# Spectral FFN on one core: the first pair of batch 0 fed from SBUF, mix weights loaded ahead of the stores, weight bands decoded one pair later

## Chip, cores and metric

One core of one Trainium2 chip. The metric is the device time of one execution in microseconds (us), the median of several runs. Engines are named as in the profile: PE (TensorE), DVE (VectorE), ACT (ScalarE), POOL (GpSimd), SP (SyncE, which here only issues transfers).

## What is computed

Shapes: x is (8, 3008, 256) float32; w_r and w_i are 256 x 256; b_r and b_i have 256 elements; the two weights of the feed-forward part, 256 x 2048 and 2048 x 256, arrive as float64.

```python
X = rfft(x, axis=1);  Xr, Xi = X.real, X.imag
Yr = Xr @ w_r - Xi @ w_i + b_r
Yi = Xr @ w_i + Xi @ w_r + b_i
Yr, Yi = soft threshold of each with 0.01
y  = irfft(Yr + 1j * Yi, n=3008, axis=1)          # (8, 3008, 256)
h  = y.reshape(24064, 256) @ moe_w_in
out = (h * clip(h + 3, 0, 6) / 6) @ moe_w_out
```

## The kernel before

The transform of length 3008 = 64 x 47 is done in two steps. Stage 1 is a 47-point transform as matmuls with a constant matrix (f47), for all 64 residues; its result `a` goes to a scratch array in DRAM, scr1. The middle stage takes two of the 24 frequencies at a time (a "pair", `g`, 12 in all), reads their 128 rows (64 residues, real and imaginary) back from scr1, and does: `s2`, the 64-point transform; `s3`, the mix with w_r and w_i, where each operand is split into a high and a low part (`taken` makes X's high part on ACT, `remainder` the low part on DVE) and a first product adds the bias through a mean matrix; the threshold; `s5`, the inverse 64-point transform, whose result goes to scr2. The inverse 47-point transform and the feed-forward part follow in "units" of rows, with the middle stages of later batches spread between.

The two feed-forward weights arrive as pairs of 32-bit words of float64 and are decoded on chip in 16 "bands" (even: w_in, odd: w_out), each of 512 KB, in the steps exponent, clamped, sign, middle, rest, upper, lower or folded, sums_hi, sums_lo. `band()` issues a band's load on SP, `stage(n, what)` does one step of band n on DVE, ACT or POOL, and `tick` does the first two. EARLY bands are done during batch 0's middle stage, the rest in `later()`.

Around the change, the program does this:

- `first_stage1` (L325) handles batch 0 in seven sets, one of 96 rows and six of 120. Per set: sum and difference of the loaded halves on DVE and POOL (L347, L348), two products on PE (L358), a copy of each result to `a` (L371 on ACT, L369 on DVE), and a store of each to scr1 on SP's queue (L373, fourteen in all).
- Then w_r and w_i are loaded (L709, by the helper at L151), and half of the bias (L711); `next(mid)` twice issues the constants and data of pairs 0 and 1 (`constants`, `data`, L425 to L430): 64-point matrices `f`, and `bt`, which reads scr1 back.
- Bands 0 and 1 are loaded, `warm(8)` puts eight matmuls on zeros into PE's queue, ACT splits the mix weights (casts at L130, L724 to L726), and `run(mid)` runs all pairs of `first_middle` (L417).
- `later()` (L1153) is a generator that the main loop advances at a list of slots, `fill(q)`, four slots to a unit; `lay(segment(0, 2), ...)` and `stage1(1)` are placed by slots too.

Every engine runs its instructions in program order, and each has its own list; SP's list is the queue of nearly all transfers. A transfer is given one of eight semaphores in turn, and its issue waits until the transfer that used that semaphore before has landed (DMAHW0 to DMAHW7 in the rows below). In the main part a planner sets the order of the work from slots and data, so the order listing shows it better than the code.

Of the kernel before, what the change touches and what calls it, by code (L numbers as in the profile page):

```python
# [51 lines left out]

def constants():
# [23 lines left out]

    g64 = np.zeros((2, N1, 2, N1))
# [9 lines left out]
    for k in (0, N1 // 2):  # L88
# [5 lines left out]
        "f64": f(f64, P, NK * P),  # L94
        "g64": f(g64, P, P),
# [6 lines left out]
def spectral_ffn(ctx: ExitStack, tc: tile.TileContext, x, w_r, w_i, bias, w_in, w_out, f47, f64, g64, g64u, sgn, out):  # L102
# [183 lines left out]
    EARLY = 14  # L286
# [38 lines left out]
    def first_stage1():  # L325
# [24 lines left out]

        added(0)
        added(1)
        for i, (n1, n) in enumerate(sets):
# [63 lines left out]
    def first_middle():  # L417
# [13 lines left out]

        def s2(g):
            d, f = bt.pop(g)
# [12 lines left out]
        def taken(g):  # L446
            if g % 2 == 0:
                xt[g // 2] = space([P, 2, 2, 2, 2, P], F32R, "X", "gs")
            t = xt[g // 2][:, g % 2]
            nc.scalar.copy(out=t[:, 0], in_=ps_x[g].rearrange("p (h r c) -> p h r c", h=2, r=2))  # L450

        def remainder(g):
            t = xt[g // 2][:, g % 2]
            ps = ps_x.pop(g).rearrange("p (h r c) -> p h r c", h=2, r=2)
# [72 lines left out]
        constants(0)  # L527
        data(0)
        yield
# [3 lines left out]
        for g in range(NG + 2):  # L533
            n = g + 1 if g < NG else -9
# [11 lines left out]
            if g == 0:  # L546
                tick(g)
            elif g <= NG:
                stage(g, "clamped")
            stage(n - 3, "sums_hi")  # L550
            if g <= NG:
                stage(n - 3 if g < NG else g - 2, "upper")
            if g == 1:
                stage(0, "sign")
                stage(0, "middle")
                signed(0)
            if g:
# [4 lines left out]
            if g:  # L562
                on(signed, g)
                stage(n - 1, "middle")
# [9 lines left out]
            if g == NG + 1:  # L574
                tick(NG + 1, False)
                ahead.work(1)
                ahead.work(2)
                tick(NG + 2, False)
# [123 lines left out]
    next(first)  # L702
    warm(2)
# [9 lines left out]
    next(mid)  # L713
# [6 lines left out]
    warm(8)  # L720
# [432 lines left out]
    def later():  # L1153

        band()
        stage(EARLY, "exponent")
        stage(EARLY, "clamped")
        band()
        ahead.store()
        last = len(todo_bands) - 1  # L1160
        for steps in (
            ((12, "sums_hi"),),
            ((12, "sums_lo"),),
            ((14, "sign"), (14, "middle")),
# [5 lines left out]
            ((last, "exponent"), (last, "clamped")),  # L1170
            ((last, "sign"), (last, "middle")),
            ((last, "rest"), (last, "upper"), (last, "lower")),
# [168 lines left out]
```

## Time and profile before

| | us |
|---|---|
| median of 3 runs (2577.03 to 2577.23) | 2577.08 |
| the profiled execution, whole | 2578.3 |
| its span on the core | 2576.5 |
| PE busy in the span | 2558.8 (99%) |
| DVE busy | 1956.9 (76%) |
| ACT busy | 1964.1 (76%) |
| POOL busy | 729.2 (28%) |

How to read it: PE is busy in all but some 18 us of the span, and 91% of the chain of work that ended last is PE's. A busy sum does not say where the rest lies, so the rows further down are taken from single stretches. Times in rows are us from the span's start unless marked; "x4" after an operation is a count; "[0.52 <-PE ps_a L358]" means that the engine was idle 0.52 us before it and that PE's work on that tile ended the wait.

### The profile page before, as it was taken

The page shows a single profiled execution, that of the slowest core. Times are in us where ns is not written, and L with a number is a line of the kernel's source. Part 1 is how long each engine was busy: PE and PEld are TensorE (multiplying, and loading weights), DVE is VectorE, ACT ScalarE, POOL GpSimd, SP SyncE. Part 2 cuts the span into 40 slices and gives each one's busy share as a digit, 9 for nine tenths or more (in the row PEclk, how much of TensorE's full clock was granted, in tenths as well). Part 3 has the DMA queues.
Part 4 walks back from the last instruction along what each step waited for, and adds up shares of the span by engine and source line. Part 5 has one row for each costly group of instructions (what it writes and reads, how often), then busy time and mean ns, then how long its engine had stood idle before and what let it go on. Part 6 is the DMA issues. An engine that isn't in the chain of part 4 may idle for free.

```text
span 2576.5 us, 45563 instructions
## 1 busy us (share of the span) xinstructions
PE 2558.8 (99%) x16510; PEld 2291.1 (89%) x16510; DVE 1956.9 (76%) x3176; ACT 1964.1 (76%) x4329; POOL 729.2 (28%) x716
## 2 busy tenths in 40 slices
PE   9999999999999999999999999999999999999999
PEld 6788889889999989988899888998989999999998
DVE  6888877777777877777777777787777777766676
ACT  5777777777777777777777777777777777777877
POOL 2223422333133321433313432133411221121210
PEclk9999999999999999999999999999999999999999
DMA  8534422232122221222212322222311121110000
GB/s 278 170 99 137 126 73 74 84 89 76 54 83 79 89 80 51 81 83 82 79 55 78 90 87 67 69 73 85 90 62 53 55 73 49 37 32 25 20 17 17
DMA packets 147321, 199.75 MB, mean 78 GB/s; under 512 B 16319, under 2 KB 102039, under 8 KB 147095
## 3 DMA queue, kind: packets, MB, share of 16 engines
q1 hardware_dynamic: 147095, 196.83, 25.3%
q8 instruction: 130, 2.13, 0.3%
q14 instruction: 96, 0.79, 0.1%
HBM read 99.77 MB, written 74.97 MB: 68 GB/s over the span
## 4 chain that ended last, share of the span: by engine, by line
PE 91%; DVE 3%; ACT 3%; issue 2%; DMA 2%; POOL 0%; SPq 0%; ACTq 0%; DVEq 0%; POOLq 0%
PE po L137 38%; PE ps_a L137 25%; PE pb L137 19%; PE ps_a L868 3%; PE ps_a L754 3%; PE ps_a L471 1%; DVE gs L1096 1%; ACT gs L1095 1%; DMA qt<-scr 1%; ACT r L1090 1%; DVE h L1011 0%; DMA xin<-in_x 0%; DVE r L1092 0%; PE ps_a L506 0%; PE pb L438 0%
## 5 line engine op out<-in xcount | busy, mean ns | idle before, releaser
L137 PE MATMUL po<-gs,w_out_hi 128*128 128x512 f32 x3008 | 948.4, 396 | 1.0 <-DVE gs L1096 0.8
L1090 ACT ACTIVATE r<-h,three 128x512 f32<-128x512 f32 x750 | 541.4, 724 | 149.8 <-DVE h L1011 134.9
L1092 DVE SCALAR_TENSOR_TENSOR r<-r,h 128x1024 f32<-128x1024 f32 x375 | 491.2, 1310 | 210.0 <-ACT r L1090 209.0
L137 PEld LDWEIGHTS po<-gs,w_out_hi 128*128 128x128 f32 x3008 | 565.0, 188 | 87.3 <-DVE gs L1096 3.8
L137 PE MATMUL po<-gs,w_out_lo 128*128 128x512 f32 x1504 | 611.5, 407 | 0.2 <-ACT gs L1095 0.2
L1096 DVE TENSOR_TENSOR gs<-r,gs 128x1024 fp32r<-128x1024 f32 x375 | 479.0, 1277 | 162.3 <-ACT gs L1095 162.0
L1095 ACT CAST gs<-r 128x512 fp32r<-128x512 f32 x750 | 429.0, 619 | 176.5 <-DVE r L1092 171.9
L137 PE MATMUL pb<-yb,w_in_hi 128*128 128x256 f32 x3004 | 563.5, 280 | 0.0
L137 PEld LDWEIGHTS pb<-yb,w_in_hi 128*128 128x128 f32 x3004 | 460.0, 188 | 33.5
L131 POOL TENSOR_TENSOR yb<-T,yb 128x256 fp32r<-128x256 f32 x184 | 192.2, 1046 | 853.0 <-ACT yb L130 852.7
L137 PE MATMUL ps_a<-yb,w_in_hi 128*128 128x256 f32 x2252 | 432.0, 280 | 0.0
L137 PE MATMUL pb<-yb,w_in_lo 128*128 128x256 f32 x1502 | 423.0, 282 | 3.0 <-ACT u L1008 1.7
L1011 DVE TENSOR_TENSOR h<-ps_a,u 128x256 f32<-128x256 f32 x752 | 313.7, 417 | 132.8 <-PE ps_a L137 129.6
L137 PEld LDWEIGHTS ps_a<-yb,w_in_hi 128*128 128x128 f32 x2252 | 345.0, 188 | 17.0 <-DVE yb L131 0.2
L1008 ACT COPY u<-pb 128x256 f32<-128x256 f32 x752 | 278.9, 372 | 101.7 <-PE pb L137 100.1
L137 PE MATMUL ps_a<-yb,w_in_lo 128*128 128x256 f32 x1126 | 317.6, 282 | 4.0 <-DVE h L1011 3.7
L137 PEld LDWEIGHTS pb<-yb,w_in_lo 128*128 128x128 f32 x1502 | 282.8, 188 | 41.5 <-ACT p L1008 3.1
L137 PEld LDWEIGHTS po<-gs,w_out_lo 128*128 128x128 f32 x1504 | 283.5, 188 | 20.1 <-issue 2.2
L137 PEld LDWEIGHTS ps_a<-yb,w_in_lo 128*128 128x128 f32 x1126 | 211.6, 188 | 26.8 <-DVE h L1011 10.2
L1008 ACT COPY p<-pb 128x256 f32<-128x256 f32 x376 | 138.6, 369 | 37.3 <-PE pb L137 35.6
L1011 DVE TENSOR_TENSOR h<-ps_a,p 128x256 f32<-128x256 f32 x376 | 156.3, 416 | 2.5 <-ACT p L1008 1.9
L1067 ACT COPY h<-pb 128x256 f32<-128x256 f32 x376 | 141.6, 377 | 3.4 <-PE pb L137 3.3
(189 smaller groups left out, 3370.0 us busy)
## 6 DMA issues: line engine op xcount, KB each, us to landing
xin<-in_x SPq DMA_DIRECT2D x48, 512.0 KB, 3.6
bt<-scr SPq DMA_DIRECT2D x96, 256.0 KB, 3.2
scr<-pt SPq DMA_DIRECT2D x96, 256.0 KB, 2.0
out<-ot SPq DMA_DIRECT2D x93, 256.0 KB, 2.0
scr<-a SPq DMA_DIRECT2D x96, 240.0 KB, 2.5
qt<-scr SPq DMA_DIRECT2D x96, 240.0 KB, 3.4
zt<-tc SPq DMA_DIRECT2D x336, 64.0 KB, 2.0
f<-in_f SPq DMA_DIRECT2D x96, 128.0 KB, 2.9
```

Source lines behind the costliest of these rows:

```text
L131: (on or nc.vector).tensor_tensor(out=lo, in0=src, in1=hi.bitcast(F32), op=ALU.subtract)
L137: nc.tensor.matmul(out=ps, lhsT=a, rhs=b, start=start and n == 0, stop=stop and n == len(todo) - 1, skip_group_check=more,)
L471: nc.tensor.matmul(out=to, lhsT=x[:, xh, dh, which], rhs=w_s[w][wh][:, dh * D : (dh + 1) * D], start=False, stop=n == 2 and (which, dh) == ...
L754: nc.tensor.matmul(out=psv[:, dh, :, u, :], lhsT=data[:, u, dh * P : (dh + 1) * P], rhs=f[:, u, :], start=True, stop=True,)
L868: nc.tensor.matmul(out=ps[:, cs * w + g * rows : cs * w + (g + 1) * rows], lhsT=qt[:rows, cs, g, dh * P : (dh + 1) * P], rhs=f47_s[2][:row ...
L1008: nc.scalar.copy(out=t, in_=ps)
L1011: nc.vector.tensor_tensor(out=hs[i][:, u, half * H : (half + 1) * H], in0=ps, in1=keep.pop((i, n)), op=ALU.add)
L1067: nc.scalar.copy(out=hs[i][:, 1, :H], in_=pb)
L1090: nc.scalar.activation(out=r[:, u], in_=h[:, u], func=AF.Relu, bias=three, scale=1.0)
L1092: nc.vector.scalar_tensor_tensor(out=r, in0=r, scalar=6.0, in1=h, op0=ALU.min, op1=ALU.mult)
L1095: nc.scalar.copy(out=t[:, 0, u], in_=r[:, u])
L1096: nc.vector.tensor_tensor(out=t[:, 1], in0=r, in1=t[:, 0].bitcast(F32), op=ALU.subtract)
```

## The change

1. `first_rows()` gives the row order of the seven sets, `f64d` is a new constant of 256 KB with the 64-point matrices of the first pair in that order. `direct(i, a)` copies frequencies 0 and 1 of set i from `a` into the tile `bt_first`, both in SBUF, in two transfers on ACT's queue, issued behind ACT's first copy of the next set. `s2_first` multiplies them, each frequency on its own half of the rows and into its own PSUM bank, and X of pair 0 is made in two halves. Pair 0's constants and data are no longer loaded.
2. The loads of f_first (from f64d), w_r, w_i and half of the bias are issued ahead of the fourteen stores.
3. `warm(8)` becomes `warm(3)`. `tick` and the band steps in the middle stage come one pair later; EARLY goes from 14 to 13, so that `later()` starts with three bands' loads and has more steps and slots; the first slot of `stage1(1)` moves from 4 to 12.

```diff
         added(1)
+        behind_by_one = None
         for i, (n1, n) in enumerate(sets):
...
+                if behind_by_one is not None:
+                    direct(i - 1, behind_by_one)
+                    behind_by_one = None
                 dst = scr1[0][c, n1 : n1 + n].rearrange("(g j) k d -> (j k) g d", g=w // D)
                 nc.sync.dma_start(out=dst, in_=a[:, c].rearrange("p (g d) -> p g d", d=D))
+            behind_by_one = a
+            if i + 1 == len(sets):
+                direct(i, a)
...
+        def direct(i, a):
+            at, rows, w = first_rows()[i][0], *shapes[i]
+            for u in range(2):
+                src = a[u:rows:NK].rearrange("p c (g d) -> p c g d", d=D)
+                to = slice(u * N1 + at, u * N1 + at + rows // NK)
+                nc.scalar.dma_start(out=bt_first[to, :, : w // D], in_=src)
...
+        def s2_first():
+            pss = [room(True)[:, :D], ps_o.tile([P, 512], F32, name="po1")[:, :D]]
+            ps_x[0] = [ps.rearrange("p (h r c) -> p h r c", h=2, r=2) for ps in pss]
+            for dh in range(2):
+                for c in range(2):
+                    for gr in range(2):
+                        for u, ps in enumerate(pss):
+                            rows = slice(u * N1, u * N1 + (len(SEGS) - 1) * J + (0 if gr else SEGS[-1][1]))
+                            nc.tensor.matmul(
+                                out=ps[:, dh * P : (dh + 1) * P],
+                                lhsT=bt_first[rows, c, gr, dh * P : (dh + 1) * P],
+                                rhs=f_first[rows, 2 * c + gr, :],
...
-        constants(0)
-        data(0)
-        yield
...
-            if g == 0:
-                tick(g)
-            elif g <= NG:
-                stage(g, "clamped")
+            if g == 1:
+                tick(0)
+            elif 1 < g <= NG:
+                stage(g - 1, "clamped")
...
     next(first)
+    bt_first = space([P, 2, 2, D], F32, "bt_first", "z")
+    f_first = space([P, 4, P], F32, "f_first", "e")
+    nc.sync.dma_start(out=f_first, in_=f64d.rearrange("p (k c) -> p k c", c=P))
+    w_re, w_im = [loaded(w, P, 2 * D, n, "ot") for w, n in ((w_r, "w_r"), (w_i, "w_i"))]
+    nc.sync.dma_start(out=bias_s[: P // 2], in_=bias[: P // 2])
     warm(2)
...
     for i in range(len(SEGS)):
         next(first)
-    w_re, w_im = [loaded(w, P, 2 * D, n, "ot") for w, n in ((w_r, "w_r"), (w_i, "w_i"))]
...
-    nc.sync.dma_start(out=bias_s[: P // 2], in_=bias[: P // 2])
...
-    warm(8)
+    warm(3)
...
-    EARLY = 14
+    EARLY = 13
...
-        band()
-        stage(EARLY, "exponent")
-        stage(EARLY, "clamped")
-        band()
+        for _ in range(3):
+            band()
         ahead.store()
-        last = len(todo_bands) - 1
         for steps in (
+            ((12, "rest"), (12, "upper")),
             ((12, "sums_hi"),),
             ((12, "sums_lo"),),
+            ((13, "exponent"), (13, "clamped")),
+            ((14, "exponent"), (14, "clamped")),
+            ((13, "sign"), (13, "middle")),
...
-    for q in (0, 6, 8, 9, 11, 13, 15, 17, 18, 19, 20, 22, 45):
+    for q in (0, 3, 5, 6, 8, 9, 10, 11, 13, 14, 16, 17, 19, 20, 21, 23, 45):
...
-    for q in (4, 21, 23, 25, 27):
+    for q in (12, 21, 23, 25, 27):
```

How it moves instructions, at three places. The first is ACT in stage 1, from its first copy to the first cast of the mix weights, with the waits of each; before:

```order
L371 COPY a<-ps_a 96x256 [waits PE_49]
L371 COPY a<-ps_a 120x512 [waits PE_49] x4
L371 COPY a<-ps_a 120x512 [waits DMAHW1_49,DMAHW0_49,PE_49]
L371 COPY a<-ps_a 120x512 [waits DMAHW3_49,DMAHW2_49,PE_49]
L371 COPY a<-pb 120x512 [waits PE_49]
L130 CAST w_r_hi<-cst 128x512 [waits DMAHW6_49]
```

and now:

```order
L390 COPY a<-ps_a 120x512 [waits DMAHW1_49,DMAHW0_49,PE_49]
L367 DMA bt_first<-a 5x1024 [waits DMAHW6_49,DVE_49,Activation_49]
L367 DMA bt_first<-a 5x1024 [waits DMAHW1_49]
L390 COPY a<-ps_a 120x512 [waits DMAHW7_49,DMAHW4_49,PE_49]
L367 DMA bt_first<-a 5x1024 [waits DMAHW2_49,DVE_49,Activation_49]
L367 DMA bt_first<-a 5x1024 [waits DMAHW4_49]
L390 COPY a<-pb 120x512 [waits PE_49]
L367 DMA bt_first<-a 5x1024 [waits DMAHW5_49,Activation_49]
L367 DMA bt_first<-a 5x1024 [waits DMAHW0_49]
L141 CAST w_r_hi<-cst 128x512
L141 CAST w<-cst 128x512
```

Fourteen transfers (L367) stand between the copies (L371 before, L390 now); each waits for a transfer that used its semaphore before, and the first of each two for DVE and ACT's copies too. The casts of the mix weights come behind the last two.

The second is SP's list in the same stretch, again with waits; before, from the last stores of `a` to the read-back of pair 1 (`cst` are the loaded mix weights, `scr_96` is scr1):

```order
L373 DMA scr_96<-a 120x2x256 [waits DMAHW3_49,DVE_49]
L373 DMA scr_96<-a 120x2x256 [waits DMAHW4_49,Activation_49]
L373 DMA scr_96<-a 120x2x256 [waits DMAHW5_49,Activation_49]
L151 DMA cst<-in_w_r 128x512 [waits DMAHW6_49]
L151 DMA cst<-in_w_i 128x512 [waits DMAHW7_49]
L711 DMA bias<-in_bias 64x512 [waits DMAHW0_49]
L427 DMA f_214<-in_f 128x256 [waits DMAHW1_49]
L430 DMA bt<-scr_96 128x512 [waits DMAHW4_49,DMAHW5_49,DMAHW3_49,DMAHW2_49]
L427 DMA f_218<-in_f 128x256
L430 DMA bt<-scr_96 128x512
```

and now, from the last loads of x to the fourth store (`f_first` is the new constant):

```order
L348 DMA xin<-in_x 128x1024 x6
L756 DMA f_first<-in_f64d 128x512 [waits DMAHW2_49]
L162 DMA cst<-in_w_r 128x512 [waits DMAHW3_49]
L162 DMA cst<-in_w_i 128x512 [waits DMAHW5_49]
L758 DMA bias<-in_bias 64x512 [waits DMAHW6_49]
L395 DMA scr_96<-a 96x256 [waits DMAHW0_49,Activation_49]
L395 DMA scr_96<-a 96x256 [waits DMAHW1_49,DVE_49]
L395 DMA scr_96<-a 120x2x256 [waits DMAHW2_49,Activation_49]
L395 DMA scr_96<-a 120x2x256 [waits DMAHW4_49,DVE_49]
```

The four loads stand between the loads of x and the stores, each behind the landing of an earlier load, and pair 0's `f` and `bt` are gone.

The third is the change-over from the middle stage to the main phase: SP's list from the first loads of scr2 for the inverse transform's segments (`qt`, `front`) on, where `st` are the bands; before:

```order
L850 DMA qt<-scr_212 120x2x256 x2
L846 DMA front<-scr_212 48x2x256
L850 DMA qt<-scr_212 120x2x256 x2
L208 DMA st<-in_w_in 128x1024
L208 DMA st<-in_w_out 128x1024
L415 DMA scr_117<-a 120x2x256 x4
L850 DMA qt<-scr_212 120x2x256 x2
```

and now:

```order
L903 DMA qt<-scr_229 120x2x256 x2
L899 DMA front<-scr_229 48x2x256
L903 DMA qt<-scr_229 120x2x256 x2
L219 DMA st<-in_w_out 128x1024
L219 DMA st<-in_w_in 128x1024
L219 DMA st<-in_w_out 128x1024
L440 DMA scr_129<-a 120x2x256 x4
L903 DMA qt<-scr_229 120x2x256 x2
```

A third band stands ahead of the last pair of qt loads shown, which is segment 2's. On PE, the products of that segment (L868 before, L921 now, `f_all,qt`) and what stands ahead of them, where L137 and L148 are products of the first unit; before:

```order
L137 MATMUL ps_a<-yb,w_in_lo 128x256
L137 MATMUL pb<-yb,w_in_hi 128x256
L137 MATMUL ps_a<-yb,w_in_hi 128x256 x2
L137 MATMUL pb<-yb,w_in_lo 128x256
L137 MATMUL pb<-yb,w_in_hi 128x256 x2
L137 MATMUL pb<-yb,w_in_lo 128x256
L137 MATMUL pb<-yb,w_in_hi 128x256 x2
L137 MATMUL pb<-yb,w_in_lo 128x256
L137 MATMUL pb<-yb,w_in_hi 128x256 x2
L868 MATMUL ps_a<-f_all,qt 128x120 x2
L137 MATMUL ps_a<-yb,w_in_lo 128x256
```

and now:

```order
L148 MATMUL pb<-yb,w_in_lo 128x256
L148 MATMUL pb<-yb,w_in_hi 128x256 x2
L148 MATMUL pb<-yb,w_in_lo 128x256
L148 MATMUL pb<-yb,w_in_hi 128x256 x2
L148 MATMUL pb<-yb,w_in_lo 128x256
L148 MATMUL pb<-yb,w_in_hi 128x256 x2
L148 MATMUL ps_a<-yb,w_in_lo 128x256
L148 MATMUL ps_a<-yb,w_in_hi 128x256 x2
L148 MATMUL pb<-yb,w_in_lo 128x256
L148 MATMUL pb<-yb,w_in_hi 128x256 x2
L921 MATMUL ps_a<-f_all,qt 128x120 x2
L148 MATMUL ps_a<-yb,w_in_lo 128x256
```

Three groups of three more of the unit's products stand ahead of that segment's first product now.

## Rows read from the trace of the kernel before

**Rows 1.** Windows: from:to, us, busy of PE, PEld, DVE, ACT, POOL, clock, DMA, GB/s

```profile
15.00:20.00 5.00, 5.00 (x11) 1.85 (x12) 2.37 (x4) 1.80 (x4) 2.54 (x2) 1.00 0.93 310
45.00:90.00 45.00, 45.00 (x353) 40.57 (x351) 42.07 (x75) 35.00 (x75) 13.73 (x22) 1.00 0.73 241
```

**Rows 2.** Chain of waits, start and us of each piece, 19 to 34 us

```profile
19.91 0.59 ACT a L371
20.52 2.85 DMA scr<-a
23.44 3.78 DMA bt<-scr
27.36 1.13 PE pb L438 x8
28.49 0.86 PE po L695 x2
29.37 0.50 PE ps_a L461
29.86 2.87 PE ps_a L471 x24
32.74 0.91 PE pb L438 x8
```

**Rows 3.** DMA issues of 0 to 30 us: KB each, median us to landing

```profile
scr<-a SPq DMA_DIRECT2D x12, 240.0 KB, 4.3
```

**Rows 4.** Timeline of SP and ACT: start, us, engine, line, operation, idle before

```profile
20.89 0.45 SPq L151 DMA_DIRECT2D cst<-in_w_r  x1
...
24.88 0.62 ACT L130 CAST w_r_hi<-cst 128x512 fp32r<-128x512 f32 x1 [4.39 <-DMA cst<-in_w_r]
25.88 0.62 ACT L130 CAST w<-cst 128x512 fp32r<-128x512 f32 x1 [0.39 <-DMA cst<-in_w_i]
...
28.79 0.57 ACT L450 CAST X<-pb 128x512 fp32r<-128x512 f32 x1
```

**Rows 5.** Timeline of PE in the first 40 us

```profile
1.54 3.78 PE L695 MATMUL pb<-blank 128*128 128x512 f32 x4 [1.54 <-DVE blank L699]
...
19.70 7.11 PE L695 MATMUL pb<-blank 128*128 128x512 f32 x16
...
38.59 0.38 PE L506 MATMUL ps_a<-tc,signs 64*128 64x256 f32 x1
38.60 0.38 PE L506 MATMUL po<-tc,signs 64*128 64x256 f32 x1
```

**Rows 6.** Page, DMA issues of the whole span: the transfers within SBUF

```profile
zt<-tc SPq DMA_DIRECT2D x336, 64.0 KB, 2.0
```

**Rows 7.** Change-over: chain of waits, and PE's timeline at segment 2's first product

```profile
101.18 8.28 DMA qt<-scr
...
112.33 0.37 PE pb L137 x3
...
109.59 0.68 PE L868 MATMUL ps_a<-f_all,qt 120*128 120x120 f32 x4 [0.32 <-DMA qt<-scr]
```

**Rows 8.** Decode steps at the change-over: one window, then DVE's and ACT's timeline

```profile
97.43:100.87 3.44, 2.92 (x21) 2.21 (x19) 3.30 (x9) 2.53 (x6) 0.00 (x0) 1.00 1.03 232
...
95.17 0.42 DVE L215 TENSOR_SCALAR t<-st 128x512 int32<-128x512 int32 x1
...
95.63 0.72 ACT L218 ACTIVATE t<-t,less 128x512 int32<-128x512 int32 x1 [0.19 <-DVE t L215]
...
98.61 0.70 ACT L230 ACTIVATE st<-st 128x512 f32<-128x512 int32 x1
99.93 0.51 ACT L261 CAST w_in_hi<-t 128x384 fp32r<-128x384 f32 x1 [0.62 <-DVE t L241]
```

**Rows 9.** Windows of the main phase's first units, columns as in rows 1

```profile
110.00:150.00 40.00, 38.59 (x235) 32.70 (x233) 36.03 (x64) 30.80 (x71) 9.43 (x11) 1.00 0.24 74
150.00:190.00 40.00, 39.88 (x236) 32.97 (x235) 29.95 (x50) 31.09 (x67) 7.98 (x10) 1.00 0.38 109
```

More of the change, by code (lines that the diff above doesn't have):

```diff
@@ L50, in positions, with first_rows @@
     return np.concatenate(order)
+def first_rows():
+    return [((len(SEGS) - 1) * J, *SEGS[-1]), *((J * i, *seg) for i, seg in enumerate(SEGS[:-1]))]
 def constants():
@@ L76, in constants @@
     f64[1, :, :, 1] = -c64[:, None] * sign.T[None]
+    rows = [(at + j, n1 + gr * J + j, gr) for at, n1, n in first_rows() for gr in range(-(-n // J)) for j in range(min(n, J))]
+    f64d = np.zeros((2, N1, 2, 2, 2, N1))
+    for row, n, gr in rows:
+        f64d[:, row, :, gr] = f64[:, n, :2].transpose(1, 0, 2, 3)
     g64 = np.zeros((2, N1, 2, N1))
@@ L94, in constants @@
         "f64": f(f64, P, NK * P),
+        "f64d": f(f64d, P, 4 * P),
         "g64": f(g64, P, P),
@@ L101, in spectral_ffn @@
 @with_exitstack
-def spectral_ffn(ctx: ExitStack, tc: tile.TileContext, x, w_r, w_i, bias, w_in, w_out, f47, f64, g64, g64u, sgn, out):
+def spectral_ffn(ctx: ExitStack, tc: tile.TileContext, x, w_r, w_i, bias, w_in, w_out, f47, f64, f64d, g64, g64u, sgn, out):
     nc = tc.nc
@@ L430, in data @@
             nc.sync.dma_start(out=bt[g][0], in_=src[:, 2 * g : 2 * g + 2, :])
+        def s2_first():
[10 more added lines that the diff above has]
+                                rhs=f_first[rows, 2 * c + gr, :],
+                                start=(c, gr) == (0, 0),
+                                stop=(c, gr) == (1, 1),
+                            )
         def s2(g):
+            if g == 0:
+                return s2_first()
             d, f = bt.pop(g)
@@ L449, in taken @@
             t = xt[g // 2][:, g % 2]
+            if g == 0:
+                for u, ps in enumerate(ps_x[0]):
+                    nc.scalar.copy(out=t[:, 0, :, :, u * N1 : (u + 1) * N1], in_=ps)
+                return
             nc.scalar.copy(out=t[:, 0], in_=ps_x[g].rearrange("p (h r c) -> p h r c", h=2, r=2))
@@ L453, in remainder @@
             t = xt[g // 2][:, g % 2]
+            if g == 0:
+                for u, ps in enumerate(ps_x.pop(0)):
+                    hi, lo = (t[:, n, :, :, u * N1 : (u + 1) * N1] for n in range(2))
+                    nc.vector.tensor_tensor(out=lo, in0=ps, in1=hi.bitcast(F32), op=ALU.subtract)
+                return
             ps = ps_x.pop(g).rearrange("p (h r c) -> p h r c", h=2, r=2)
@@ L533, in first_middle @@
         for g in range(NG + 2):
-            n = g + 1 if g < NG else -9
+            n = g if 0 < g < NG else -9
             on(s2, g)
@@ L545, in first_middle @@
                 on(stored, g - 2)
-            if g == 0:
-                tick(g)
-            elif g <= NG:
-                stage(g, "clamped")
+            if g == 1:
+                tick(0)
+            elif 1 < g <= NG:
+                stage(g - 1, "clamped")
             stage(n - 3, "sums_hi")
             if g <= NG:
-                stage(n - 3 if g < NG else g - 2, "upper")
-            if g == 1:
+                stage(n - 3 if g < NG else g - 3, "upper")
+            if g == 2:
                 stage(0, "sign")
                 stage(0, "middle")
+            if g == 1:
                 signed(0)
-            if g:
+            else:
                 stage(n - 1, "sign")
@@ L563, in first_middle @@
                 on(signed, g)
+            if g > 1:
                 stage(n - 1, "middle")
@@ L1169, in later @@
             ((13, "rest"), (13, "upper"), (13, "lower")),
-            ((last, "exponent"), (last, "clamped")),
-            ((last, "sign"), (last, "middle")),
-            ((last, "rest"), (last, "upper"), (last, "lower")),
+            ((15, "exponent"), (15, "clamped")),
+            ((15, "sign"), (15, "middle")),
+            ((15, "rest"), (15, "upper"), (15, "lower")),
         ):
```

5 lines of the change are left out of this document (2 added, 3 removed).

## Prediction, made before the change was run

> **What bounds the kernel now.** I read the windows first: they say where a microsecond on an engine is a microsecond of the end. In 45 to 90 us, the first middle stage, PE is busy 45.00 of 45.00 us [rows 1]. Its share there and, nearly, in the rest of the kernel means that the only time to win or lose lies where PE waits: the start, the change-over to the main phase, and the first units behind it.
>
> The chain of waits shows the start. After the last stage-1 copy (19.91 us) PE has no real work until 27.36: the last store takes 2.85 us from issue to landing, the read-back 3.78 us, then come eight products (1.13 us), two warming ones (0.86), the mean product (0.50), and the mix products begin at 29.86 [rows 2]. The change goes at the two transfers. In the same stretch the transfer engines are full: 0.93 busy in 15 to 20 us at 310 GB/s [rows 1], and stores of 240 KB take 4.3 us from issue to landing [rows 3]. Landings of successive full stores stand 0.68 us apart there, an estimate from 240 KB at about 360 GB/s, somewhat above that window's mean. So a byte that is added or put ahead here delays all behind it.
>
> On ACT, the weight casts begin at 24.88 after 4.39 us of waiting for w_r [rows 4]; that wait the early loads remove.
>
> **The change, part by part.** *Start, transfers.* Four loads go ahead of the stores: f_first 256 KB, w_r 256, w_i 256, half of the bias 128, together 896 KB, 2.55 us at 360 GB/s. The direct transfers add 256 KB, about 0.65 us before the store that matters. Nothing of the read-back's 256 KB or f(0)'s 128 KB comes before that point, so these savings help only behind it.
>
> *Start, the queues.* The order of ACT shows what is new: fourteen transfers stand between the copies, and each waits on a semaphore that another transfer, on either queue, used eight transfers before. The order of SP shows the same for the four loads: each must wait for one of the seven xin loads. ACT runs in order, so a held direct transfer holds the copies of the next set, the stores of these copies, and in the end the weight casts. The last direct transfer waits for the 12th of 14 stores. Before, the last store landed at 20.52 + 2.85 = 23.37 [rows 2], the 12th at 23.37 - 2 x 0.68 = 22.0. Now: 22.0 + 2.55 + 0.65 = 25.2 us. The nearest transfer from SBUF to SBUF is zt<-tc, 64 KB in 2.0 us [rows 6], so the data are there at 27.2, where the products began at 27.36 before: the removed round trip is nearly eaten up.
>
> *First pair's products.* 16 matmuls with 64 and 60 rows instead of four with 128 (32 instructions against 8 in the trace, which counts two for one). The two halves sit on different halves of the array and write different banks, as the two products L506 do that begin at 38.59 and 38.60 [rows 5]. I count 16 pairs x 0.125 us = 2.0 us against 1.13, an estimate from 1.13 / 8 = 0.14 us an instruction, a little less for 128 columns each. Bounds: 1.1 us if halves cost half, 4.0 if they do not run side by side; the rows at 38.6 speak for the former pairing. So PE ends them at 29.2 (28.49 before): **+0.7 us**. Is ACT late? Its weight casts took 28.79 - 24.88 - 0.39 = 3.5 us [rows 4]; from 25.4 they end at 28.9. The two half casts of X cost at most 0.57 each [rows 4], 30.3 at the end from 29.2, and the mix products want X at 29.2 + 0.86 + 0.50 = 30.6: covered, by 0.3 us. The second pair's read-back starts when the last store has landed, 23.37 + 3.2 = 26.6, and lands by 26.6 + 3.78 = 30.4; PE wants it at 30.6 + 2.87 = 33.4. Covered. Warming products go from 8 to 3, all in time in which PE waits [rows 5]: nothing. Bounds of this term: if no direct transfer is ever held, the last two are issued by 20.5 + 0.9 (0.45 us an issue, as SP's [rows 4]), land at 22.95, and the mix products begin at 26.3, 3.6 us sooner, less if the second read-back then is late: -3.6. Upper bound +2.1, worked out with the third rival.
>
> *Pairs.* The decode steps slide by one pair in a stretch in which PE has no idle time [rows 1]; they cost nothing while DVE keeps within its 42.07 of 45 us, and one pair's less work there leaves it more room.
>
> *Change-over.* A third band of 512 KB stands ahead of segment 2's qt loads. The chain's longest piece there is such a qt load, 101.18 to 109.46, and PE waited 0.32 us for it [rows 7]. 512 KB at 360 GB/s are 1.46 us more. The order of PE puts nine more matmuls ahead of the first qt product: 0.37 / 3 us each [rows 7], 1.1 us of work moved into the wait. **+0.4 us**. Bounds: -0.2 (the wait was not full and is filled better) to +1.4 (the nine find their inputs late).
>
> *Main phase.* Sign, rest and folded steps, DVE's 3.30 us of 97.43 to 100.87 and 0.42 for the exponent [rows 8], about 3.8 us with gaps, leave the change-over and come after 105 us; on ACT 0.72 + 0.70 + 0.51 = 1.9 us [rows 8]. What does a microsecond of DVE cost PE there? In 110 to 150 us PE idles 1.41 us with DVE at 36.03 of 40; in 150 to 190 it idles 0.12 with DVE at 29.95 [rows 9]. That is 1.29 / 6.08 = 0.21 us of PE per us of DVE, times 3.8: **+0.8 us**. Bounds: 0 if the gaps take it all, 3.8 + 1.9 = 5.7 if none do.
>
> Sum: +0.7 + 0.4 + 0.8 = +1.9 us on the profiled 2578.3, that is 2580.2. The profiled run stands 1.2 us above the median of the three runs, so I forecast **2579.0 us** against 2577.08. A change under 0.2% (5.15 us) counts as none: below 2571.9 or above 2582.2 would count.
>
> **The rivals** (times as a median again, so 2578.3 - 1.2 plus the sum). *Directs never held (faster).* ACT keeps its pace, the transfers land with the copies. The start gains 3.6 us, or 2.3 if the second pair's read-back lands only at 30.4 (32.74 before [rows 2]); I take 3.0. -3.0 + 0.4 + 0.8 = -1.8: 2575.3. For it: a wait on a transfer that has long landed costs nothing, and the first sets' transfers may meet only such. Against it: the transfer engines are full until 33 us, and the queue order ties the last one to the 12th store.
>
> *Decode on PE's path (slower).* Place: 110 to 150 us. DVE has 3.97 us free of 40 there and gets 3.8; ACT has 9. The gate's steps pass between ACT and DVE, so a decode step in front of one delays the next product, and PE has no other unit to fill in. It decides as soon as the units that are ready are used up. Price at the upper bound: 0.7 + 0.4 + 5.7 = +6.8, 2583.9. For it: DVE would be full. Against: with DVE at 90% PE still idled only 3.5% of the window.
>
> *Direct transfers use few of the transfer engines.* The nearest row, zt<-tc, moves 64 KB in 2.0 us [rows 6], 32 GB/s, and cannot tell. Were all twelve 20 KB transfers on the same five engines, 240 KB would be 48 KB on each, where a full store is 15 KB on each of 16 and takes 0.68 us: 2.0 to 2.2 us in place of 0.65, so +1.4 on the start (its bound, +2.1): 2580.4. The Trainium skill, "DMA: Bandwidth & Descriptors", section "Why a DMA increments its semaphore by 16 and not by 1", says that a transfer is spread over the largest number of engines up to 16 that divides the slowest dimension of both sides, the lowest-numbered ones: five here. No row of this trace shows a transfer of five partitions.
>
> *Clock.* PE is quiet before the first pair, and three warming products may not bring it up. The first four, after 1.5 us of nothing, take 3.78 us, 0.95 each; the sixteen of the wait 7.11, 0.44 each [rows 5], half and full clock, 1.2 and 2.4 GHz, though the granted column reads 1.00. If 2.3 us of the first pair's work runs at the lower level it takes 4.6, which costs 2.3 on top of the forecast: 2581.3. The Trainium skill, "TensorE: Matmul & The Clock Gate", Part 1, has the same two levels; the durations here agree with it, the column does not show it. Against it: stage 1's products, stretched by a held ACT, keep PE at work until some 3 us before.
>
> **How the numbers follow.** Forecast 0.43; directs not held 0.19; five engines 0.12; clock 0.10; decode on the path 0.16. The range goes from the second case with its own best ends (-3.6 - 0.2 + 0.8 = -3.0: 2574.1) to the clock's case with the change-over 0.9 worse (2582.2), and leaves out most of the slow rival and a little at the lower end. Faster by over 0.2% needs gains that no bound holds: 0.02. Slower: three quarters of the slow rival and 0.02 of sums of the others, 0.14. Within 0.2%: 0.84.
>
> **What would show it.** Right: gaps before ACT's direct transfers from the fourth set on and stretched copies, the last issue near 25.2 us; the first pair's products from 27.2, for 2.0 us; mix products near 30.6; no wait for the second read-back; segment 2's qt about 1.4 us later; PE idle in 110 to 150 up from 1.4 to about 2.2. Wrong: the last issue near 21 us (the faster rival); directs taking over 3 us each to land (five engines); first-pair products of twice the length (clock); PE idle over 5 us in 110 to 150 (decode).

## The result, and the profile after

The change made the kernel slower: 2592.05 us against 2577.15 (medians of six runs each), a ratio of 1.0057 with a 95% interval of 1.0044 to 1.0069. The forecast was 2579.0 in a range of 2574.1 to 2582.2, so the time lies 10 us above its upper end. The profiled execution took 2592.24 us, with a span of 2590.5 against 2576.5.

The 14.0 us of span can be laid out stage by stage, by four marks, instructions that both programs have: the mean product that opens a pair (second and last pair), and the first product of the gate (`gs<-r,gs`) of the first and of the sixteenth unit. PE's timeline of before, then DVE's:

```profile
33.39 0.48 PE L461 MATMUL ps_a<-w_m_hi,w_m_lo 128*128 128x512 f32 x1
86.74 0.50 PE L461 MATMUL ps_a<-w_m_hi,w_m_lo 128*128 128x512 f32 x1
...
114.32 1.23 DVE L1096 TENSOR_TENSOR gs<-r,gs 128x1024 fp32r<-128x1024 f32 x1 [0.19 <-ACT gs L1095]
...
216.79 1.23 DVE L1096 TENSOR_TENSOR gs<-r,gs 128x1024 fp32r<-128x1024 f32 x1
```

And the same four of after:

```profile
41.44 0.48 PE L513 MATMUL ps_a<-w_m_hi,w_m_lo 128*128 128x512 f32 x1
96.47 0.50 PE L513 MATMUL ps_a<-w_m_hi,w_m_lo 128*128 128x512 f32 x1
...
126.19 1.45 DVE L1149 TENSOR_TENSOR gs<-r,gs 128x1024 fp32r<-128x1024 f32 x1
...
230.94 1.23 DVE L1149 TENSOR_TENSOR gs<-r,gs 128x1024 fp32r<-128x1024 f32 x1
```

The delays are 8.05, 9.73, 11.87 and 14.15 us. So the start lost 8.05 us, the pairs 1.7, the change-over 2.1 and the first sixteen units 2.3; after that the delay stays between 12.7 and 15.0 us to the end. The border between the last two stages is rough, as the gate is a step of DVE's and other DVE work moves around it; PE's idle time between the marks grows by 1.6 us in the change-over (2.12 to 3.70) and by 1.85 in the sixteen units (1.63 to 3.48). Each of the four stages is over the forecast's term for it (0.7, 0, 0.4, 0.8).

The chain of waits of after shows the start; it answers to [rows 2]:

```profile
20.38 4.17 DMA scr<-a
...
24.57 0.69 ACTq L367
...
25.30 0.59 ACT a L390
...
25.92 0.69 ACTq L367
...
26.65 2.25 DMA bt_first<-a
...
35.13 2.00 PE po L746 x2
37.13 0.43 PE ps_a L513
37.56 3.23 PE ps_a L523 x24
```

By this chain the data are there at 28.9, where the read-back let the products begin at 27.36. Then the first pair's products run until 35.13, 6.2 us in place of 1.13, the two warming products and the mean product take 2.43 in place of 1.36, and the mix 3.23 in place of 2.87. Data, products, these three and the mix make 1.6 + 5.1 + 1.1 + 0.4 us of the 8.05. PE's timeline shows how the products run; it answers to [rows 5]:

```profile
18.95 3.39 PE L746 MATMUL pb<-blank 128*128 128x512 f32 x6
28.92 0.55 PE L465 MATMUL pb<-f_first,bt_first 34*128 34x128 f32 x1 [6.58 <-DMA bt_first<-a]
...
33.60 0.58 PE L465 MATMUL pb<-f_first,bt_first 34*128 34x128 f32 x1
33.61 0.58 PE L465 MATMUL po<-f_first,bt_first 34*128 34x128 f32 x1
33.98 0.42 PE L465 MATMUL pb<-f_first,bt_first 34*128 34x128 f32 x1
33.99 0.42 PE L465 MATMUL po<-f_first,bt_first 34*128 34x128 f32 x1
```

The three warming products end at 22.3, and PE is idle for 6.58 us. Pairs of instructions, one on each half, then start some 0.36 us apart, three times what I had counted. The windows of after (columns as in [rows 1]) show why a part of that is the clock:

```profile
20.00:25.00 5.00, 2.25 (x4) 0.59 (x4) 0.00 (x0) 1.17 (x2) 0.00 (x0) 0.96 0.94 286
25.00:30.00 5.00, 1.08 (x6) 0.89 (x6) 1.29 (x2) 3.00 (x6) 0.00 (x0) 0.50 0.64 167
30.00:35.00 5.00, 5.00 (x29) 3.49 (x28) 1.09 (x2) 0.99 (x3) 0.00 (x0) 0.50 0.93 320
35.00:40.00 5.00, 5.00 (x24) 3.81 (x23) 0.76 (x2) 0.65 (x2) 0.00 (x0) 0.67 0.27 72
```

The granted clock goes to 0.50, the lower of the two levels (1.2 GHz against 2.4), at about 24.6, in PE's idle stretch, and stays there until about 38.3. The Trainium skill, "TensorE: Matmul & The Clock Gate", Part 1, names these two levels; here the column shows both.

ACT's timeline shows the held transfers; the cast answers to [rows 4]:

```profile
20.66 0.58 ACT L390 COPY a<-ps_a 120x512 f32<-120x512 f32 x1 [3.23 <-DMA bt_first<-a]
20.76 2.42 ACTq L367 DMA_DIRECT2D bt_first<-a  x2
...
25.92 1.42 ACTq L367 DMA_DIRECT2D bt_first<-a  x2
27.38 0.62 ACT L141 CAST w_r_hi<-cst 128x512 fp32r<-128x512 f32 x1 [1.49 <-DMA bt_first<-a]
```

Two issues that wait for nothing take 1.42 us, 0.7 each, where I had taken 0.45; the other pairs take up to 3.46, as they are held. At the change-over, SP's timeline has

```profile
108.35 0.43 SPq L219 DMA_DIRECT2D st<-in_w_out  x1
111.44 0.36 SPq L219 DMA_DIRECT2D st<-in_w_in  x1
...
114.47 2.19 SPq L903 DMA_DIRECT2D qt<-scr  x2
```

SP stands from 108.8 to 111.4 at the second of the three bands, until a decode step of POOL ends (`w_out_lo`, L280), and segment 2's loads are queued behind it. That segment's first product comes at 122.42 instead of 109.59, 12.8 us late, where the last pair was 9.7 late.

### The profile page after: what moved, and what is told of

Its sections match the earlier page's. It is cut to its first block, busy times and chain, and to the rows that moved or that the text cites. A ratio compares the mean times of both kernels' runs of the same rounds, so it can differ in the third digit from the quotient of the medians.

```text
span 2590.5 us, 45628 instructions
## 1 busy us (share of the span) xinstructions
PE 2563.5 (99%) x16524; PEld 2294.4 (89%) x16524; DVE 1962.8 (76%) x3177; ACT 1962.2 (76%) x4330; POOL 730.7 (28%) x716
## 3 DMA queue, kind: packets, MB, share of 16 engines
q1 hardware_dynamic: 146951, 196.70, 25.2%
## 4 chain that ended last, share of the span: by engine, by line
PE 89%; DVE 4%; ACT 3%; issue 2%; DMA 1%; POOL 0%; SPq 0%; ACTq 0%; DVEq 0%; POOLq 0%
PE po L148 38%; PE ps_a L148 25%; PE pb L148 19%; PE ps_a L921 3%; PE ps_a L807 3%; DVE gs L1149 1%; DVE r L1145 1%; DVE h L1064 1%; ACT gs L1148 0%; DMA xin<-in_x 0%; ACT r L1143 0%; PE ps_a L523 0%; DVE st L245 0%; POOL st L268 0%; DVE w_in_lo L292 0%
## 5 line engine op out<-in xcount | busy, mean ns | idle before, releaser
L148 PE MATMUL po<-gs,w_out_hi 128*128 128x512 f32 x3008 | 948.6, 396 | 1.5 <-DVE gs L1149 1.4
L148 PEld LDWEIGHTS po<-gs,w_out_hi 128*128 128x128 f32 x3008 | 564.7, 188 | 87.3 <-DVE gs L1149 4.0
L148 PE MATMUL po<-gs,w_out_lo 128*128 128x512 f32 x1504 | 610.4, 406 | 0.3 <-ACT gs L1148 0.2
L148 PE MATMUL pb<-yb,w_in_hi 128*128 128x256 f32 x3004 | 564.0, 280 | 0.0
L148 PEld LDWEIGHTS pb<-yb,w_in_hi 128*128 128x128 f32 x3004 | 460.2, 188 | 33.6 <-issue 0.2
L148 PE MATMUL ps_a<-yb,w_in_hi 128*128 128x256 f32 x2252 | 431.9, 280 | 0.0
L148 PE MATMUL pb<-yb,w_in_lo 128*128 128x256 f32 x1502 | 423.1, 282 | 4.1 <-ACT p L1061 2.2
L148 PEld LDWEIGHTS ps_a<-yb,w_in_hi 128*128 128x128 f32 x2252 | 344.8, 188 | 17.2 <-issue 0.2
L148 PE MATMUL ps_a<-yb,w_in_lo 128*128 128x256 f32 x1126 | 318.9, 283 | 4.2 <-DVE h L1064 3.6
L148 PEld LDWEIGHTS pb<-yb,w_in_lo 128*128 128x128 f32 x1502 | 282.8, 188 | 42.7 <-ACT p L1061 4.3
L148 PEld LDWEIGHTS po<-gs,w_out_lo 128*128 128x128 f32 x1504 | 283.5, 188 | 19.8 <-issue 1.8
L148 PEld LDWEIGHTS ps_a<-yb,w_in_lo 128*128 128x128 f32 x1126 | 211.6, 188 | 28.6 <-DVE h L1064 11.7
L142 POOL TENSOR_TENSOR yb<-raw,yb 128x256 fp32r<-128x256 f32 x138 | 130.4, 954 | 47.4 <-ACT yb L141 47.4
```

Of the source, the lines that this page charges most:

```text
L142: (on or nc.vector).tensor_tensor(out=lo, in0=src, in1=hi.bitcast(F32), op=ALU.subtract)
L148: nc.tensor.matmul(out=ps, lhsT=a, rhs=b, start=start and n == 0, stop=stop and n == len(todo) - 1, skip_group_check=more,)
```

## The experiments

The kernel before was run again beside each group; its medians there were 2577.6 to 2577.9. A median's interval is about 2.6 us wide on either side, so where two experiments are only 2 us apart, the delays at the four marks decide. They come from one profiled execution each, but what a stage costs repeats: in the six programs with the changed kernel's steps in the pairs, these cost 1.68 to 1.74 us.

**The head alone, the decode alone, the loads alone.** `e2_head_only` takes of the change all but the decode's part (EARLY, the pairs' steps, `later`, the slots stay as before).

```diff
-    EARLY = 13
+    EARLY = 14
-            n = g if 0 < g < NG else -9
+            n = g + 1 if g < NG else -9
...
```

> The changed kernel's head (transfers within SBUF, early loads, three warming products) with the decode schedule of before. Theory (the later decode costs by itself, about 6.3 us: 2.0 in the pairs, 2.2 up to the first unit, 2.3 in the first units): the mix products begin at 37.6 as in the changed kernel, the delay stays near 7.7 us from there on, the time is about 2585. Rival (the losses behind the head are the late head's own consequence): the delay grows to 14 us as before, about 2592.

Measured: 2587.02 us, ratio 1.0036 (1.0022 to 1.0049). The delay is 9.1 us at the second pair and 9.3 at the sixteenth unit: what the head loses at the start, it neither gains nor loses up to there. It lost 1 us more at the start than in the changed kernel, as the clock came back later (the mix took 4.42 us instead of 3.23).

`e3_decode_only` has the rest:

```diff
-    EARLY = 14
+    EARLY = 13
-            n = g + 1 if g < NG else -9
+            n = g if 0 < g < NG else -9
...
```

> The kernel before with only the later decode: steps one pair later, 13 early bands, three bands ahead of segment 2's loads, the new slots. Theory (it costs by itself about 6.3 us): about 2583.5, with SP held at the third band and segment 2's loads some 3 us later. Rival (no cost of its own): 2577 to 2578.

Measured: 2584.21 us, ratio 1.0025 (1.0014 to 1.0035). Delays at the four marks: 0.4, 2.1, 4.75, 7.2 us. The decode's move has its own price in each of the three later stages, without the head. Head and decode apart make 9.3 + 7.2 = 16.5 us, 2.3 more than the whole change; 1 us of that is the head's later clock, the rest I did not trace. SP's timeline shows the same hold as in the changed kernel, at the second band and not at the third:

```profile
100.68 0.43 SPq L208 DMA_DIRECT2D st<-in_w_out  x1
103.84 0.36 SPq L208 DMA_DIRECT2D st<-in_w_in  x1
...
107.95 1.98 SPq L852 DMA_DIRECT2D qt<-scr  x2
```

`e4_early_loads` moves only w_r, w_i and half of the bias ahead of the stores.

```diff
     next(first)
+    w_re, w_im = [loaded(w, P, 2 * D, n, "ot") for w, n in ((w_r, "w_r"), (w_i, "w_i"))]
+    nc.sync.dma_start(out=bias_s[: P // 2], in_=bias[: P // 2])
     warm(2)
...
     for i in range(len(SEGS)):
         next(first)
-    w_re, w_im = [loaded(w, P, 2 * D, n, "ot") for w, n in ((w_r, "w_r"), (w_i, "w_i"))]
...
```

> The kernel before with only the loads of w_r, w_i and half of the bias moved ahead of the stores; no transfers within SBUF. Theory (the same bytes stand ahead of the first pair's read-back in either order, and SP's waits for the loads of x are hidden by the full transfer engines): within 1 us of 2577. Rival (SP's list stands at these waits, stores start at 13 instead of 7 us and the read-back comes later): 2579 or more.

Measured: 2577.69 us, ratio 1.0 (0.9991 to 1.001); mix products 0.4 us earlier in the first pair, 0.2 later from the fourth on. The order of these loads alone is worth nothing. That they stood in the read-back's way before and stand in the stores' way now is an argument; the run shows only the sum.

**The clock.** `e1_warm11` and `e5_warm8` change one line of the changed kernel.

```diff
-    warm(3)
+    warm(11)
```

> The changed kernel with eleven warming products behind stage 1 instead of three, so that PE is at work from 19 us until about 28.5. Theory (PE's idle 6.6 us let the clock fall, and the first pair's products ran at 1.2 GHz): the granted clock stays 1.00, the first pair's products take about 3 us instead of 6.2, the mix products begin near 33.5 instead of 37.6, the time is about 2588. Rival (the products are slow by themselves, as the two halves do not run side by side): they still take 6 us and the time stays at 2592.

Measured: 2592.85 us, ratio 1.0057 (1.004 to 1.0074). Theory and rival were each half right. PE's timeline:

```profile
19.65 12.86 PE L746 MATMUL pb<-blank 128*128 128x512 f32 x22
...
33.16 0.37 PE L465 MATMUL pb<-f_first,bt_first 30*128 30x128 f32 x1
33.17 0.37 PE L465 MATMUL po<-f_first,bt_first 30*128 30x128 f32 x1
33.37 0.27 PE L465 MATMUL pb<-f_first,bt_first 30*128 30x128 f32 x1
33.38 0.27 PE L465 MATMUL po<-f_first,bt_first 30*128 30x128 f32 x1
```

At a granted clock of 1.00 the pairs start 0.207 us apart and the products take 3.6 us (32.56 to 36.17) instead of 6.2. But the warming products held PE until 32.5. In this run the last data landed at 30.1, as stage 1's last product began at 18.69 instead of 17.99; PE was 2.5 us late for them, and the two together ate what the clock gave back: the delay at the second pair is 7.6 us instead of 8.05.

`e5_warm8` has eight warming products, as before the change.

```diff
-    warm(3)
+    warm(8)
```

> The changed kernel with eight warming products as before the change. In the run with eleven the granted clock stayed 1.00 and the first pair's products took 3.6 us, but the last warming product ended only at 32.6, 3.7 us after the data; 22 instructions took 12.9 us, so 16 take 9.4 and end near 29.0, where the data land. Theory (the clock is worth some 3.5 us if PE is free in time): mix products near 33.7, time 2588.5. Rival (something other than PE holds the mix products until 37, as both runs had them there): 2592.

Measured: 2591.53 us, ratio 1.0052 (1.0037 to 1.0067). The products began at 30.34, after an idle 1.19 us, and the delay at the second pair is 7.0 us instead of 8.05: a gain of 1 us, not of 3.5. From the first of these products to the first mix product it took 5.8 us instead of 8.4; the data came 1.4 us later, as stage 1 was 0.9 us later in this run. Windows of the products and of what follows them:

```profile
30.30:33.00 2.70, 2.66 (x24) 2.05 (x24) 1.27 (x3) 1.72 (x5) 0.00 (x0) 1.00 0.72 175
33.00:36.10 3.10, 3.10 (x15) 1.71 (x12) 0.81 (x3) 0.65 (x2) 0.00 (x0) 0.66 1.00 377
```

The products ran at 1.00, and then the clock fell with PE busy in all of 33.0 to 36.1; the warming and mean products behind them paid for it. The 1.19 us of idle time may have had a part in that fall. `e10_change_mended`, below, has the same eight products and an idle time of 0.05 us; its clock fell all the same, from 33.5 to 36.9, just after the products, and its delay at the second pair is 6.0 us. With eleven it did not fall. So covering the gap did not keep the clock each time.

**Do the halves run side by side?** `e12_halves_apart` is `e1_warm11` with the loop over the halves outermost.

```diff
-            for dh in range(2):
-                for c in range(2):
-                    for gr in range(2):
-                        for u, ps in enumerate(pss):
+            for u, ps in enumerate(pss):
+                for dh in range(2):
+                    for c in range(2):
+                        for gr in range(2):
```

> The changed kernel with eleven warming products (clock 1.00 throughout) and the first pair's products ordered by half, all sixteen instructions of one half of the array ahead of the other's. Theory (the two halves never ran side by side to any use; 0.207 us for a pair of instructions is two times 0.104): the products still take about 3.5 us. Rival (side by side they saved half): about 6.5 us, or 32 times 0.207.

One execution, 2599.33 us. PE's timeline, then the windows of the two halves (columns as in [rows 1]):

```profile
31.43 3.38 PE L465 MATMUL pb<-f_first,bt_first 34*128 34x128 f32 x16
34.74 5.44 PE L465 MATMUL po<-f_first,bt_first 34*128 34x128 f32 x16
```

```profile
31.40:34.70 3.30, 3.27 (x16) 2.35 (x16) 0.00 (x0) 0.00 (x0) 0.00 (x0) 1.00 0.97 332
34.70:40.10 5.40, 5.40 (x17) 3.68 (x16) 0.42 (x1) 0.37 (x1) 0.00 (x0) 0.55 0.32 86
```

My theory fell. Sixteen instructions of one half alone take 3.31 us (31.43 to 34.74) at full clock, 0.207 each, and the other sixteen 5.44 us, as the clock fell during them. So the halves do run side by side; but an instruction on half of the rows takes 0.207 us when the next is on the same half, where one on all 128 rows took 1.13 / 8 = 0.14 or less [rows 2]. The Trainium skill, "TensorE: Matmul & The Clock Gate", Part 3, says that a weight load overlaps products under way only on other rows. That fits the two half orders, 0.104 us an instruction alternating and 0.207 not, since every instruction here loads its own weights; that the full-height ones run faster than 0.207 it does not explain, and no run separates load from product.

**The transfers.** `e8_head_late_loads` is the head alone with w_r, w_i and the bias behind the stores again and six warming products instead of three, two edits at once.

```diff
-    w_re, w_im = [loaded(w, P, 2 * D, n, "ot") for w, n in ((w_r, "w_r"), (w_i, "w_i"))]
-    nc.sync.dma_start(out=bias_s[: P // 2], in_=bias[: P // 2])
     warm(2)
...
     for i in range(len(SEGS)):
         next(first)
+    w_re, w_im = [loaded(w, P, 2 * D, n, "ot") for w, n in ((w_r, "w_r"), (w_i, "w_i"))]
+    nc.sync.dma_start(out=bias_s[: P // 2], in_=bias[: P // 2])
...
-    warm(3)
+    warm(6)
```

> The change's head alone without the early loads: w_r, w_i and half of the bias behind the stores as before, the transfers within SBUF kept, six warming products (12 instructions, 7 us, until 26.7). Theory (640 KB ahead of the stores delay the transfers within SBUF by 1.8 us, and the clock stays up): data at 27.1, products until 30.7, mix products near 32, the time about 2579.5 against 2587 for the whole head. Rival (the weights then come last, their casts after 28 us hold the mix products until 34): 2582 or more.

Measured: 2584.49 us, ratio 1.0029 (1.0017 to 1.0041), delay 6.1 us. The data were there by 27.80, 1.1 us sooner, but the products took 5.0 us and not 3.6, as the clock fell to 0.51 in 30 to 35 us. The gain over `e2_head_only` is 3.0 to 3.3 us at the four marks, and the run does not say how much of it is the loads and how much the warming; the theory's 7.5 needed a clock that stays up. The rival had the time, but not its reason: no cast held the mix products.

`e11_head_sp_directs` is the head alone with the transfers within SBUF on SP's queue, each set's behind its own stores, with the weights behind all stores and four warming products. One of its lines:

```diff
...
-                nc.scalar.dma_start(out=bt_first[to, :, : w // D], in_=src)
+                nc.sync.dma_start(out=bt_first[to, :, : w // D], in_=src)
...
```

> The change's head with the weights behind the stores and the transfers within SBUF on SP's queue, behind the stores of their set, so that ACT issues none; four warming products. Theory (held issues on ACT delay the copies, and with them all that follows): ACT's last copy near 20.5 us as before the change, data near 25 to 26, mix products near 31 to 32, about 2580. Rival (SP's own list is held the same way, 28 issues in a row): last copy on time, but data near 28 and the time as with late loads, 2584.

Measured: 2587.19 us, ratio 1.0039 (1.0024 to 1.0054). The rival was right on the data and 3 us short on the time; the granted clock was 0.50 in 30 to 35 us here too. ACT's last copy, SP's last issues of the transfers, and PE's first product of the pair:

```profile
18.86 0.59 ACT L389 COPY a<-pb 120x512 f32<-120x512 f32 x1 [0.47 <-PE pb L376]
...
23.12 1.42 SPq L367 DMA_DIRECT2D bt_first<-a  x2
24.65 0.89 SPq L391 DMA_DIRECT2D scr<-a  x2
25.59 1.42 SPq L367 DMA_DIRECT2D bt_first<-a  x2
...
28.48 0.55 PE L459 MATMUL pb<-f_first,bt_first 34*128 34x128 f32 x1 [5.25 <-DMA bt_first<-a]
```

With no copy held, the data are there at 28.48, hardly sooner. Fourteen issues of 0.71 us, 10 us in all, stand in the list, against 0.45 for a store. On either queue the data come later than by the read-back (27.36).

**The decode's three costs.** `e6_spares_even` is the decode alone, with the spare steps of the middle stage in even pairs:

```diff
-            next(spare, None) if g % 2 and g < NG or g == NG else None
+            for _ in range((0 < g <= NG and g % 2 == 0) + (g == NG)):
+                next(spare, None)
```

> The kernel before with the later decode, and the spare steps of the middle stage (DVE work of 0.4 to 1.5 us, in odd pairs) put into even pairs. Theory (the shift by one pair put the spare steps into the pairs whose decode is heavy, and left the wait for POOL's and ACT's folding uncovered, 0.8 us in every second pair): the pairs lose nothing any more, 2.1 us less than with the decode alone, about 2582.1. Rival (DVE is simply over its budget): 2584.

Measured: 2582.17 us, ratio 1.0015 (1.0006 to 1.0024). The pairs' delay is gone: -0.2 us at the second pair and at the last. It is 1.1 us at the first unit and 3.5 at the sixteenth, so the change-over costs less too. Two of DVE's four waits with the decode alone, and none like them with the spares moved, where the longest is

```profile
69.28 0.56 DVE L281 TENSOR_TENSOR w_in_lo<-t,w_in_hi 128x384 fp32r<-128x384 f32 x1 [0.82 <-ACT w_in_hi L261]
80.50 0.56 DVE L281 TENSOR_TENSOR w_in_lo<-t,w_in_hi 128x384 fp32r<-128x384 f32 x1 [0.81 <-ACT w_in_hi L261]
```

```profile
74.88 0.69 DVE L488 SCALAR_TENSOR_TENSOR tc<-ps_a,tc 128x512 f32<-128x512 f32 x1 [0.43 <-ACT tc L486]
```

Bands of w_in and w_out alternate, and a w_in band's fold goes from DVE over POOL and ACT back to DVE. Before, the spare step lay on DVE during that trip. One pair later it lay in the other pair: DVE waits 0.8 us in one and is overfull in the next. Theory and rival were 2 us apart in time; the delay at the pairs speaks for the theory.

`e7_bands_late` is the decode alone with one band ahead of segment 2's loads and two behind:

```diff
-        for _ in range(3):
-            band()
+        band()
...
+            if steps == ((12, "sums_hi"),):
+                band()
+                band()
```

> The kernel before with the later decode, but only band 13 loaded ahead of segment 2's loads and bands 14 and 15 behind them. Theory (SP stands 2.7 us at band 14's load, whose buffer band 11's decode still holds, and the bytes of two bands take 2.9 us): segment 2's first product 3 to 5 us earlier than with the decode alone, the time about 2580.5, if the first units do not then wait for band 14. Rival (segment 2 is not what the first units wait for, DVE's decode work is): 2584.

Measured: 2582.41 us, ratio 1.002 (1.0011 to 1.003). SP no longer stands: segment 2's loads go out at 103.91 instead of 107.95, and its first product comes at 111.86 instead of 115.34. The delay at the sixteenth unit is 5.6 us, 1.7 less. At the first unit it is 7.4, 2.65 more, as more of segment 2's work on DVE comes ahead of the gate; so the gain is sure only over both stages together. `e9_decode_both` has both edits.

> The kernel before with the later decode, spare steps in even pairs and bands 14 and 15 behind segment 2's loads. Theory (the two costs lie in different stages and add): 2584.2 less 2.0 less 1.8, about 2580.4, and what is left over 2577.9, some 2.5 us, is the decode work moved into the main phase. Rival (both runs took away the same delay): 2582.

Measured: 2581.16 us, ratio 1.0015 (1.0006 to 1.0025); the delays are 0.06, 0.05, 4.2 and 2.45 us. Of the 7.2 us at the sixteenth unit the first edit took 3.7, the second 1.7, and both 4.8: the two gains nearly add. The 2.45 us that remain are the price of the change-over and the first sixteen units together; that they are the decode work moved into the main phase is the theory, and no run separates it.

**All mended together.** `e10_change_mended` is the changed kernel with eight warming products and both edits.

> The changed kernel with eight warming products, spare steps in even pairs and bands 14 and 15 behind segment 2's loads. Theory (head and decode add): 2592.0 less about 3.8 for the decode and up to 1 for the clock, about 2587.5. Rival (behind a late head the decode's costs are hidden, or others take their place): 2590 or more.

Measured: 2589.24 us, ratio 1.0049 (1.0032 to 1.0066). The time lies between theory and rival. The delay is 6.0 us from the second pair to the last and 10.2 at the sixteenth unit, 4 us less than in the changed kernel. Behind the pairs it grows by 4.2 us where the decode with both edits alone grew by 2.4. The trace shows where: PE waited 1.63 us for segment 2's loads, and then the granted clock was at 0.50 in a stretch in which no other trace has it there:

```profile
115.41:118.82 3.41, 3.41 (x18) 3.41 (x17) 1.63 (x6) 1.38 (x4) 0.26 (x1) 0.50 0.30 117
```

Half of 3.41 us is 1.7, an estimate of what that cost, and nearly all of the 1.8. No version tried beats the kernel before.

## Why the prediction was wrong

The step that failed most is the start, +0.7 us, which measured 8.05. Its parts come first.

*Read-back and casts "covered": right.* PE waited neither for the second pair's read-back nor for ACT's casts in the first pair's path. The transfers were held, as forecast: ACT's copies waited up to 3.23 us behind them, so the faster rival is out.

*"So the data are there at 27.2": 28.9.* Three things in this step were off. The twelfth store landed at 26.1 (by the trace's semaphore records) and not at 25.2: the transfer engines moved 286 GB/s in 20 to 25 us, as they had before the change (293), and I had used 360. ACT came to the last issue only after that: its last hold, on the tenth store, ended at 24.55, and behind it came an issue, a copy and another issue (0.69, 0.59 and 0.69 us in the chain above), so that the last transfer was issued at 26.65. With issues of 0.45, as I had priced them, that would be 0.5 us sooner. And it took 2.25 us to land, not 2.0. That the small transfers use few engines was a rival, and its condition holds: in the trace each of the twelve moves as five packets of 4 KB with five landings counted on its semaphore, so on five engines at most. Eight of the twelve took over 3 us from issue to landing, its sign. What that cost the start was not separated from the rest.

*"16 pairs x 0.125 us = 2.0 us": 6.2 us.* This is the largest error, in two parts. At full clock the products take 3.6 us, as a pair costs 0.207 us. The trace before [rows 5] could only hint at it, and I read no more from it than that pairs start together; the next pair starts at

```profile
38.81 0.38 PE L506 MATMUL ps_a<-tc,signs 64*128 64x256 f32 x1
```

0.21 us later, but with 256 columns, twice as many. My bounds of 1.1 and 4.0 held that part. The other 2.6 us are the clock.

*"Warming products go from 8 to 3, all in time in which PE waits: nothing."* They kept the clock up. Removing them let it fall for the products, the warming and mean products and the start of the mix; in the changed kernel that is 2.6 us on the products, 1.1 on the warming and mean products behind them (35.13 to 37.56 against 36.17 to 37.46 with eleven) and 0.4 on the mix. The rival had this with 2.3 us and one chance in ten, and rested its doubt on stage 1 keeping PE at work until 3 us before; the idle stretch was 6.58 us. But the clock alone would not have saved the start: with eight warming products 1.0 us comes back in `e5_warm8` and 2.1 in `e10_change_mended`.

*"They cost nothing", of the pairs: 1.7 us.* I took DVE's mean load for the whole and did not ask which step covers which wait. The cost is a matter of odd and even pairs, and disappears with the spare steps moved.

*Change-over, +0.4: 2.1 us (2.6 for the decode alone).* I priced a third band's bytes and not the wait of the bands' own issues. The second of them waits for a buffer that a decode step frees; I followed the queue's bytes and not its head. Without that hold (`e7_bands_late`) segment 2's first product comes 3.5 us sooner, and 1.7 us of it are left at the sixteenth unit.

*Main phase, +0.8: 2.3 us.* The direction was right and the size was not; in `e9_decode_both` this stage and the change-over cost 2.45 us together, where I had 1.2 for both. The rate of 0.21 us came from two windows; in 120 us around the first units, before and after:

```profile
110.00:230.00 120.00, 117.68 (x737) 101.59 (x736) 100.80 (x168) 90.83 (x205) 32.40 (x35) 1.00 0.33 93
```

```profile
124.00:244.00 120.00, 115.83 (x717) 99.65 (x716) 103.48 (x170) 90.89 (x205) 31.64 (x34) 1.00 0.33 93
```

PE is idle 4.17 us instead of 2.32, with 2.68 us more of DVE: 0.69 us for each. From mark to mark (114.32 to 216.79, and 126.19 to 230.94) it is 1.85 us with 3.35 more of DVE, 0.55 for each, so the rate is rough, but over twice mine. In 110 to 150 us PE's idle time went from 1.41 to 3.28 us, between the 2.2 I had named as right and the 5 I had named as the slower rival's. In 120 to 130 us before, DVE was already busy 9.96 of 10 us: the steps came where there was no room. That this is the reason was not tried. The slower rival had that mechanism at its upper bound of 5.7.

The sum: 8.05 + 1.7 + 2.1 + 2.3 = 14.15 where 1.9 was forecast. All four errors go the same way, as each term was priced as if what it leans on (clock, cover, buffer, spare time) stayed as it was.

## What to carry to other kernels

A shorter way for data pays only if what it is made of is cheap: count its issues at their own measured price and its products at the start-to-start distance of like products, not at their bytes and columns. Filler work on a waiting engine, and steps that sit in another step's wait, are parts of the schedule; before one is taken away or shifted, ask what it covers, and whether the pattern has a period (here, odd and even pairs) that the shift breaks. Where a load is moved ahead in a queue, read what its own issue waits for, as everything behind it waits too.

## What had not been expected of the hardware

An instruction on half of PE's rows took 0.207 us where one of the same columns on all rows took 0.14 or less; two of them side by side only make up for that. The granted clock fell to 0.55 while PE was busy in 5.40 of 5.40 us (`e12_halves_apart`) and to 0.66 in `e5_warm8`, both in or just after these half-row products, and in `e10_change_mended` from 33.5 to 36.9, just after them with no gap ahead; in `e1_warm11` it stayed at 1.00 through the same products. So a busy engine in the profile did not always keep the clock. What decides that was not tried. An issue of a transfer within SBUF of five partitions took 0.7 us on ACT as on SP, against 0.45 for a store of 240 KB; it moved as five packets, one for each partition, where the trace counts fifteen landings for such a store.
